# kv, the normalizer and kv Wo of a linear-attention block in one batch of small TensorE tiles, with the token sum on DVE

## The chip, the cores and the metric

The kernel runs on one core of one Trainium2 chip. The metric is device microseconds of one execution. Engines: PE is TensorE's matmul, PEld its weight load, DVE is VectorE, ACT is ScalarE, POOL is GpSimd.

## The reference, cut to what matters

```python
# A: linear attention, S = 2048 tokens, D = 512, 32 heads of 16
q, k, v = split(x @ wqkv)                       # per head
pq, pk = phi(q), phi(k)                         # phi(t) = where(t > 0, t + 1, exp(t)) + 1e-6
kv  = einsum("bhsd,bhse->bhde", pk, v)          # 16x16 per head
z   = einsum("bhsd->bhd", pk)                   # token sum of phi(k)
num = einsum("bhqd,bhde->bhqe", pq, kv)
den = einsum("bhqd,bhd->bhq", pq, z)[..., None] + 1e-6
a   = (num / den) @ wo
# B: a token-mixing MLP on layernorm(x), F = 1792 (the bulk of the matmuls: uacc, then yps)
out = g * a + (1 - g) * b
```

The kernel never forms v. It accumulates G = x^T pk (gacc), takes kv = wv^T G per head, folds kv with Wo into W2 = kv Wo (four blocks of 128 rows), and at the end computes pq W2 (aps). In the profile, kacc and qacc are x times the k and q columns of wqkv, and denps is den.

## The kernel before, in the parts that matter

```python
def mm(o, lhsT, rhs, start, stop, **kw):           # every matmul has this one line in the profile
    nc.tensor.matmul(o, lhsT=lhsT, rhs=rhs, start=start, stop=stop, **kw)

def kv_matmuls():                                  # 32 matmuls on 128x64 tiles
    kvps = bank("kvps")
    for j in range(ND):
        for k in range(ND):
            for h in (0, H2):                      # H2 = 64
                c = slice(j * P + h, j * P + h + H2)
                mm(kvps[h : h + H2, c], wv_sb[:, k, c], gT[:, k, c], k == 0, k == ND - 1,
                   tile_position=(0, h))
    for h in (0, H2):                              # keep the 16x16 blocks on the diagonal
        d = slice(h, h + H2)
        nc.vector.tensor_tensor(out=kvbdT[d, :, d], in0=kvps[d, :]..., in1=mask[d, d]..., op=ALU.mult)

def z_matmuls():                                   # sum over tokens: 8 matmuls against ones
    zps = bank("zps")
    for j in range(ND):
        for i, part in enumerate((zhi, zlo)):      # zacc split into two bf16 parts by DVE
            mm(zps[:, 8 * j : 8 * j + 8], part[:, j * P : (j + 1) * P], ones8[:], i == 0, i == 1)
    nc.vector.tensor_tensor(out=Z32..., in0=zps..., in1=maskH..., op=ALU.mult)

def w2_matmul(j):                                  # one full 128x128 matmul, 512 wide
    wps2 = bank("wps2")
    mm(wps2[:], kvbdT[:, j, :], wo_sb[:, j, :], True, True)
    nc.scalar.activation(out=W2sb[:, j, :], in_=wps2[:], func=ACT.Copy)

def den_matmuls():                                 # 16 matmuls on 128x32 tiles, 512 wide
    ...
    nc.vector.reciprocal(out=rden[:], in_=denps[:])

for j in range(NB0, NF):                           # NB0 = 3, NF = 14: one block of the MLP each
    for t in range(NT):                            # 16 matmuls of 128x512
        mm(acc[:], w1c[c][:, t, ...], hs[:, t, :], t == 0, t == NT - 1)
    gelu(j, acc)                                   # ACT
    if j == NB0 + 2:
        z_matmuls()
    if j == NB0 + 3:
        kv_matmuls()
        den_matmuls()
        gate_sums(); rden_chunk(0); rden_chunk(1)
    if NB0 + 5 <= j < NB0 + 5 + ND:
        w2_matmul(j - NB0 - 5)
    ...
```

Of the kernel before, what the change touches and what calls it, by code (L numbers as in the profile page):

```python
# [7 lines left out]
ACT = mybir.ActivationFunctionType  # L8
ALU = mybir.AluOpType
AX = mybir.AxisListType  # L10
BF16 = mybir.dt.bfloat16
FP32 = mybir.dt.float32
# [3 lines left out]
def kernel(  # L16
# [13 lines left out]
    nc = tc.nc  # L30
    P = nc.NUM_PARTITIONS
    EPS = 1e-5
    PHI_EPS = 1e-6
    HEAD = 16
# [3 lines left out]
    S, D = X.shape  # L38
    F = B_w1.shape[1]
    NT = S // P  # L40
    ND = D // P
# [2 lines left out]
    NSC = S // SC  # L44
    TPC = SC // P
    FB = 4
    assert S == 2048 and D == 512 and F % P == 0
    w1_chunks = [(j, min(FB, NF - j)) for j in range(0, NF, FB)]

# [14 lines left out]
    def keep(shape, dtype, name):  # L64
        return persist.tile(shape, dtype, name=name, tag=name)

    def bank(name, dtype=FP32):
        return ps.tile([P, SC], dtype, name=name, tag="bank")
# [6 lines left out]
    wv_sb = keep([P, ND, D], BF16, "wv_sb")  # L75
    wo_sb = keep([P, ND, D], BF16, "wo_sb")
    pqT = keep([P, ND, S], BF16, "pqT")
    pk = keep([P, NT, D], BF16, "pk")
    uT = keep([P, NF, D], BF16, "uT")
    kvbdT = keep([P, ND, P], BF16, "kvbdT")  # L80
    W2sb = keep([P, ND, D], BF16, "W2sb")
    Z32 = keep([P, ND * 40], BF16, "Z32")
    zhi = keep([P, D], BF16, "zhi")
    zlo = keep([P, D], BF16, "zlo")
    zacc = keep([P, D], FP32, "zacc")
    ones8 = nc.const_aps.tensor(1.0, (P, 8), BF16)
    rden = keep([P, SC], BF16, "rden")
    ident = keep([P, P], BF16, "ident")
    mask = keep([P, P], BF16, "mask")
    maskH = keep([P, 8], BF16, "maskH")  # L90
    gw_b = keep([P, D], BF16, "gw_b")
    brow = keep([P, P], BF16, "brow")
    bcol = keep([P, NF + NT], FP32, "bcol")
# [13 lines left out]
    def mm(o, lhsT, rhs, start, stop, **kw):  # L107
        nc.tensor.matmul(o, lhsT=lhsT, rhs=rhs, start=start, stop=stop, **kw)  # L108

    def block_mask(m, cols, width):  # L110
        nc.gpsimd.memset(m, 1.0)
        nc.gpsimd.affine_select(
            out=m, in_=m, compare_op=ALU.is_ge, fill=0.0, base=0,
            pattern=[[-HEAD, cols], [0, width]], channel_multiplier=1,
        )
        nc.gpsimd.affine_select(
            out=m, in_=m, compare_op=ALU.is_ge, fill=0.0, base=HEAD - 1,
            pattern=[[HEAD, cols], [0, width]], channel_multiplier=-1,
        )
# [29 lines left out]
    for c, (j0, nb) in enumerate(w1_chunks):  # L149
        w = wpool.tile([P, NT, FB * P], BF16, name="w1c", tag="wc")  # L150
        w1c.append(w)
        for t0 in range(0, NT, 8) if c == 0 else (0,):
            t1 = t0 + 8 if c == 0 else NT
            nc.sync.dma_start(
                out=w[:, t0:t1, : nb * P], in_=w1_view[:, t0:t1, j0 * P : (j0 + nb) * P]
# [5 lines left out]
    nc.vector.memset(ones_f[:], 1.0)  # L161
    nc.vector.memset(mhalf[:], -0.5)
    nc.vector.memset(Z32[:], 0.0)
    nc.vector.memset(kvbdT[:], 0.0)
    nc.gpsimd.memset(ident[:], 0.0)
    nc.gpsimd.affine_select(
        out=ident[:], in_=ident[:], compare_op=ALU.not_equal, fill=1.0, base=0,
        pattern=[[-1, P]], channel_multiplier=1,
    )
    block_mask(mask[:].rearrange("p (a b) -> p a b", b=HEAD), P // HEAD, HEAD)  # L170
    block_mask(maskH[:].rearrange("p (a b) -> p a b", b=1), 8, 1)

    nc.gpsimd.memset(brow[:], 0.0)

    def load_small():
# [92 lines left out]
    def z_add(t):  # L268
        first = pk[:, 0, :] if t == 1 else zacc[:]
        nc.vector.tensor_tensor(out=zacc[:], in0=first, in1=pk[:, t, :], op=ALU.add)  # L270
# [39 lines left out]
    gT = persist.tile([P, ND, D], BF16, name="gT", tag="wk_sb")  # L310
# [6 lines left out]
    def gelu(j, acc):  # L317
        nc.scalar.activation(  # L318
            out=uT[:, j, :], in_=acc[:], func=ACT.Gelu_apprx_tanh, bias=bcol[:, j : j + 1]
        )  # L320
# [3 lines left out]
        nc.tensor.transpose(pt[:, 0:P], brow[:], ident[:])  # L324
        nc.vector.tensor_copy(out=bcol[:], in_=pt[:, 0 : NF + NT])

    H2 = P // 2

    def kv_matmuls():
        kvps = bank("kvps")  # L330
        for j in range(ND):
            for k in range(ND):
                for h in (0, H2):
                    c = slice(j * P + h, j * P + h + H2)
                    mm(
                        kvps[h : h + H2, c], wv_sb[:, k, c], gT[:, k, c], k == 0, k == ND - 1,
                        tile_position=(0, h),
                    )
        for h in (0, H2):
            d = slice(h, h + H2)  # L340
            nc.vector.tensor_tensor(
                out=kvbdT[d, :, d],
                in0=kvps[d, :].rearrange("p (j d) -> p j d", j=ND)[:, :, d],
                in1=mask[d, d].unsqueeze(1).to_broadcast([H2, ND, H2]), op=ALU.mult,
            )

    def z_split():
        nc.vector.tensor_copy(out=zhi[:], in_=zacc[:])
        nc.vector.tensor_tensor(out=zlo[:], in0=zacc[:], in1=zhi[:], op=ALU.subtract)

    def z_matmuls():
        zps = bank("zps")
        for j in range(ND):
            for i, part in enumerate((zhi, zlo)):
                mm(
                    zps[:, 8 * j : 8 * j + 8], part[:, j * P : (j + 1) * P], ones8[:],
                    i == 0, i == 1,
                )
        nc.vector.tensor_tensor(
            out=Z32[:].rearrange("p (j m) -> p j m", m=40)[:, :, 0:8],  # L360
            in0=zps[:, 0:32].rearrange("p (j m) -> p j m", m=8),
            in1=maskH[:].unsqueeze(1).to_broadcast([P, ND, 8]), op=ALU.mult,
        )

    def w2_matmul(j):
        wps2 = bank("wps2")
        mm(wps2[:], kvbdT[:, j, :], wo_sb[:, j, :], True, True)
        nc.scalar.activation(out=W2sb[:, j, :], in_=wps2[:], func=ACT.Copy)

    def den_matmuls():  # L370
        denps = bank("denps")
        for j in range(ND):
            for c in range(NSC):
                mm(
                    denps[32 * c : 32 * c + 32, :], Z32[:, 32 * j : 32 * j + 32], pqT[:, j, c * SC : (c + 1) * SC],
                    j == 0, j == ND - 1, tile_position=(0, 32 * c),
                )
        with nc.allow_low_precision(reason="the normalizer is used in bf16"):
            nc.vector.reciprocal(out=rden[:], in_=denps[:])

    NB0 = 3
# [16 lines left out]
        gelu(jj, accs[jj])  # L398
    for t in range(11, NT):
        z_add(t)  # L400
    z_split()

    def gate_sums():
        for t in range(NT):
            junk = work.tile([P, D], BF16, name="junk", tag="junk", bufs=2)
            nc.vector.tensor_tensor_reduce(  # L406
                out=junk[:], in0=xs[:, t, :], in1=gw_b[:], scale=1.0, scalar=0.0,
                op0=ALU.mult, op1=ALU.add, accum_out=gpre[:, t : t + 1],
            )
# [3 lines left out]
    def rden_chunk(c):  # L413
        if c == 0:
            nc.gpsimd.dma_start(out=rd_dram[:], in_=rden[:])
        for j in range(ND):
            rex = work.tile([P, SC], BF16, name="rex", tag="rex", bufs=4)
            src = rd_dram[32 * c + 8 * j : 32 * c + 8 * j + 8, :]
            nc.gpsimd.dma_start(out=rex[:], in_=src.unsqueeze(1).to_broadcast([8, HEAD, SC]))  # L419
            seg = pqT[:, j, c * SC : (c + 1) * SC]  # L420
            nc.vector.tensor_tensor(out=seg, in0=seg, in1=rex[:], op=ALU.mult)  # L421
# [3 lines left out]
    def load_w2(c):  # L425
        w = wpool.tile([P, NT, FB * P], BF16, name="w2c", tag="wc")
        w2c.append(w)
        for f0 in (0, NF // 2):
            f1 = f0 + NF // 2
            nc.sync.dma_start(  # L430
                out=w[:, f0:f1, :], in_=w2_view[:, f0:f1, c * SC : (c + 1) * SC]
            )

    for j in range(NB0, NF):
        c, jj = divmod(j, FB)
        acc = bank("uacc")
        for t in range(NT):
            mm(acc[:], w1c[c][:, t, jj * P : (jj + 1) * P], hs[:, t, :], t == 0, t == NT - 1)
        gelu(j, acc)
        if j == NB0 + 2:  # L440
            z_matmuls()
        if j == NB0 + 3:
            kv_matmuls()
            den_matmuls()
            gate_sums()
            rden_chunk(0)
            rden_chunk(1)
        if NB0 + 5 <= j < NB0 + 5 + ND:
            w2_matmul(j - NB0 - 5)
        if jj == FB - 1 or j == NF - 1:  # L450
            load_w2(c)

# [2 lines left out]
        out=gg[:], in0=gth[:], scalar1=0.5, scalar2=0.5, op0=ALU.mult, op1=ALU.add  # L455
    )
    nc.vector.tensor_scalar(
        out=c1[:], in0=gth[:], scalar1=-0.5, scalar2=0.5, op0=ALU.mult, op1=ALU.add
# [3 lines left out]
    for t in range(NT):  # L462
        c, tl = divmod(t, TPC)
        aps = bank("aps")
        for j in range(ND):
# [3 lines left out]
            out=a_sc[:], in_=aps[:], func=ACT.Identity,  # L469
            scale=gg[:, t : t + 1], bias=c2[:, t : t + 1],  # L470
        )
        for c0, W in ((0, D - P), (D - P, P)) if t == NT - 1 else ((0, D),):
            cs = slice(c0, c0 + W)
            yps = bank("yps")
            for f in range(NF):
# [6 lines left out]
                out=ot[:, :W], in0=yps[:, :W], scalar=c1[:, t : t + 1], in1=a_sc[:, cs],  # L482
# [35 lines left out]
```

## Time and profile before

| | before |
|---|---|
| median of 3 runs | 165.23 us (165.11 to 165.82) |
| span of the profiled run | 163.4 us |
| PE busy | 158.7 us, 97% |
| granted clock | 1.0 |

A busy share alone says little about a pipelined engine, so the chain of waits is read with it. These are the busy line of the page and its chain that ended last, by engine and then by line:

```profile
PE 158.7 (97%) x787; PEld 73.3 (45%) x801; DVE 88.3 (54%) x202; ACT 58.7 (36%) x90; POOL 18.3 (11%) x37
...
PE 95%; DMA 2%; issue 1%; ACT 0%; DVE 0%
PE uacc L108 30%; PE yps L108 29%; PE aps L108 9%; PE gacc L108 8%; PE qacc L108 8%; PE kacc L108 8%; DMA xs<-in_A_x_dram 2%; PE pt L195 1%; PE denps L108 1%; PE wps L108 1%; PE kvps L108 0%; ACT xT L199 0%; DVE ot L481 0%; PE zps L108 0%; PE pt L324 0%
```

The chain lies on PE for 95% of the span: hardly anything but PE's own stream sets the time. What a change takes out of that stream is gained, as long as PE does not start to wait for something else.

The timeline of PE around the part that is changed follows. Its columns are the start in us from the start of the span, the time covered, the engine, the line, the operation, the output and its inputs, the tile and shape, and the count. The times of matmuls overlap (one of 512 columns has 0.38 us, and the next starts 0.216 us after it), so costs are read from one start to the next; such a step of 0.216 us is called a slot.

```profile
67.83 0.17 PE L108 MATMUL zps<-const-bfloat16-1.0,zhi 128*128 128x8 bf16 x1
...
68.01 0.17 PE L108 MATMUL zps<-const-bfloat16-1.0,zlo 128*128 128x8 bf16 x1
68.04 3.61 PE L108 MATMUL uacc<-hs,w1c 128*128 128x512 bf16 x16
71.58 0.69 PE L108 MATMUL kvps<-gT,wv_sb 128*64 128x64 bf16 x32
72.20 1.05 PE L108 MATMUL denps<-pqT,Z 128*32 128x512 bf16 x16
73.18 1.04 PE L108 MATMUL uacc<-hs,w1c 128*128 128x512 bf16 x3
```

From the start of zps to the next uacc 0.21 us pass. From the start of kvps to the uacc after denps 1.60 us pass, on tiles that are 64 columns wide in kvps and 32 in denps.

The same view further on shows kv Wo, named wps here, as one full matmul between the blocks of uacc, each costing one slot of 0.216 us (80.10 to 80.32). Two of the four are shown.

```profile
80.10 0.38 PE L108 MATMUL wps<-wo_sb,kvbdT 128*128 128x512 bf16 x1
80.32 3.62 PE L108 MATMUL uacc<-hs,w1c 128*128 128x512 bf16 x16
83.77 0.38 PE L108 MATMUL wps<-wo_sb,kvbdT 128*128 128x512 bf16 x1
```

The timeline of DVE over the same stretch shows the split of z, its mask, and the two mask instructions of kv. The bracket is the idle time before an instruction and what ended it.

```profile
64.08 0.43 DVE L348 CAST zhi<-zacc 128x512 bf16<-128x512 f32 x1
64.54 0.69 DVE L349 TENSOR_TENSOR zlo<-zacc,zhi 128x512 bf16<-128x512 f32 x1
68.22 0.19 DVE L359 TENSOR_TENSOR Z<-zps,maskH 128x32 bf16<-128x32 f32 x1 [2.98 <-PE zps L108]
72.32 0.86 DVE L341 TENSOR_TENSOR kvbdT<-kvps,mask 64x256 bf16<-64x256 f32 x2 [3.91 <-PE kvps L108]
73.31 3.36 DVE L379 RECIPROCAL rden<-denps 128x512 bf16<-128x512 f32 x1
```

### The profile page before, as it was taken

To read this page: it belongs to the slowest core of one execution; us is meant where nothing else is said; L and a number is where in the kernel's file an instruction comes from. 1 tells how busy PE (TensorE), PEld (TensorE's weight loads), DVE (VectorE), ACT (ScalarE), POOL (GpSimd) and SP (SyncE) were. 2 spreads that over 40 slices of the span, in tenths; PEclk is the share of its full clock that TensorE was granted. 3 is DMA by queue.
4 is the path that set the end of the run, shared out by engine and by line. 5 is a ranking of instruction groups with operands and counts; after the bars stand their busy time and mean duration, and the time that the engine had idled before them with its cause. 6 is when DMAs were issued, how large, how long until landed. Compare 5 with 4: busy or idle time off the path is not lost.

```text
span 163.4 us, 2099 instructions
## 1 busy us (share of the span) xinstructions
PE 158.7 (97%) x787; PEld 73.3 (45%) x801; DVE 88.3 (54%) x202; ACT 58.7 (36%) x90; POOL 18.3 (11%) x37
## 2 busy tenths in 40 slices
PE   7999999999999999999999999999999999999993
PEld 2544444444444444444444444444444444444452
DVE  1599999957999999029995301156221111111112
ACT  3463386648676483111222213111112222111110
POOL 5000711200100000001055500050000000000000
PEclk9999999999999999999999999999999999999999
DMA  5999999999950007600893599932100000111001
GB/s 152 235 237 213 280 308 328 349 349 348 326 130 0 0 0 247 202 4 0 286 299 101 181 320 279 323 121 88 36 32 32 32 32 32 45 52 35 32 32 32
DMA packets 30057, 25.05 MB, mean 153 GB/s; under 512 B 7968, under 2 KB 29472, under 8 KB 30048
## 3 DMA queue, kind: packets, MB, share of 16 engines
q1 hardware_dynamic: 28032, 22.02, 45.5%
q0 software_dynamic: 1440, 2.38, 5.5%
q10 hardware_dynamic: 576, 0.52, 1.1%
q8 instruction: 6, 0.10, 0.3%
q14 instruction: 3, 0.02, 0.0%
HBM read 21.11 MB, written 2.23 MB: 143 GB/s over the span
## 4 chain that ended last, share of the span: by engine, by line
PE 95%; DMA 2%; issue 1%; ACT 0%; DVE 0%
PE uacc L108 30%; PE yps L108 29%; PE aps L108 9%; PE gacc L108 8%; PE qacc L108 8%; PE kacc L108 8%; DMA xs<-in_A_x_dram 2%; PE pt L195 1%; PE denps L108 1%; PE wps L108 1%; PE kvps L108 0%; ACT xT L199 0%; DVE ot L481 0%; PE zps L108 0%; PE pt L324 0%
## 5 line engine op out<-in xcount | busy, mean ns | idle before, releaser
L108 PE MATMUL uacc<-hs,w1c 128*128 128x512 bf16 x219 | 51.8, 379 | 0.4
L108 PE MATMUL yps<-uT,w2c 128*128 128x512 bf16 (+2 forms) x234 | 50.6, 366 | 0.2
L481 DVE SCALAR_TENSOR_TENSOR ot<-yps,c,a_sc 128x512 bf16<-128x512 f32 (+2 forms) x17 | 12.2, 720 | 46.0 <-PE yps L108 42.7
L108 PEld LDWEIGHTS <-w2c 128*128 128x128 bf16 x238 | 22.8, 98 | 25.9
L108 PEld LDWEIGHTS <-w1c 128*128 128x128 bf16 x224 | 21.7, 98 | 26.3 <-issue 0.4
L468 ACT ACTIVATE a_sc<-aps,c,gg 128x512 f32<-128x512 f32 x16 | 12.4, 778 | 46.7 <-PE aps L108 43.0
L318 ACT ACTIVATE uT<-uacc,bcol 128x512 bf16<-128x512 f32 x14 | 9.3, 687 | 28.3 <-PE uacc L108 28.3
L108 PE MATMUL aps<-W2sb,pqT 128*128 128x512 bf16 x63 | 16.4, 379 | 0.1
L108 PE MATMUL qacc<-xT,wq_sb 128*128 128x512 bf16 x63 | 16.2, 379 | 0.0
L108 PE MATMUL kacc<-wk_sb,xT 128*128 128x512 bf16 x63 | 16.0, 380 | 0.1
L108 PE MATMUL gacc<-pk,xs 128*128 128x512 bf16 x62 | 15.5, 379 | 0.1
L245 ACT ACTIVATE hs<-xs,nmr,rstd 128x512 bf16<-128x512 bf16 x16 | 12.8, 805 | 1.9 <-DVE nmr L239 1.9
L205 ACT ACTIVATE e<-qacc 128x512 bf16<-128x512 f32 x16 | 9.6, 597 | 9.2 <-PE qacc L108 8.3
L419 POOL DMA_DIRECT2D rex<-rd_dram x16 | 9.4, 602 | 23.0 <-DVE pqT L421 17.5
L205 ACT ACTIVATE e<-kacc 128x512 bf16<-128x512 f32 x16 | 9.3, 595 | 6.9 <-PE kacc L108 5.6
L209 DVE SCALAR_TENSOR_TENSOR pk<-kacc,e 128x512 bf16<-128x512 f32 x16 | 11.1, 692 | 0.6
L209 DVE SCALAR_TENSOR_TENSOR pqT<-qacc,e 128x512 bf16<-128x512 f32 x16 | 11.1, 692 | 0.6
L229 DVE BATCH_NORM_STATS2 stats<-xs 128x6 f32<-128x512 bf16 x16 | 10.9, 682 | 0.0
L206 DVE TENSOR_SCALAR e<-e 128x512 bf16<-128x512 bf16 x32 | 9.0, 282 | 3.1 <-ACT e L205 3.1
L406 DVE CUSTOM_DVE_ANT_0 junk<-xs,gw_b 128x512 bf16<-128x512 bf16 x16 | 9.9, 684 | 0.0
L270 DVE TENSOR_TENSOR zacc<-zacc,pk 128x512 f32<-128x512 f32 x14 | 9.6, 686 | 0.2
L108 PEld LDWEIGHTS <-pqT 128*128 128x128 bf16 x64 | 6.3, 98 | 7.6
(65 smaller groups left out, 69.6 us busy)
## 6 DMA issues: line engine op xcount, KB each, us to landing
w2c<-in_B_w_dram SPq DMA_DIRECT2D x8, 896.0 KB, 6.6
w1c<-in_B_w_dram SPq DMA_DIRECT2D x2, 2048.0 KB, 15.7
w1c<-in_B_w_dram SPq DMA_DIRECT2D x3, 1024.0 KB, 12.9
rex<-rd_dram POOLq DMA_DIRECT2D x16, 128.0 KB, 3.2
out_dram<-ot SPq DMA_DIRECT2D x15, 128.0 KB, 1.7
xs<-in_A_x_dram SPq DMA_DIRECT2D x3, 512.0 KB, 5.1
wq_sb<-in_A_wqkv_dram SPq DMA_DIRECT2D x1, 512.0 KB, 7.1
wv_sb<-in_A_wqkv_dram SPq DMA_DIRECT2D x1, 512.0 KB, 11.4
```

Source lines behind the costliest of these rows:

```text
L108: nc.tensor.matmul(o, lhsT=lhsT, rhs=rhs, start=start, stop=stop, **kw)
L205: nc.scalar.activation(out=e[:], in_=acc[:], func=ACT.Exp)
L206: nc.vector.tensor_scalar(out=e[:], in0=e[:], scalar1=1.0, scalar2=PHI_EPS, op0=ALU.min, op1=ALU.add)
L209: nc.vector.scalar_tensor_tensor(out=dst, in0=acc[:], scalar=0.0, in1=e[:], op0=ALU.max, op1=ALU.add)
L229: nc.vector.bn_stats(out=stats[:], in_=xs[:, t, :])
L245: nc.scalar.activation(out=hs[:, t, :], in_=xs[:, t, :], func=ACT.Identity, scale=rstd[:, t : t + 1], bias=nmr[:, t : t + 1],)
L270: nc.vector.tensor_tensor(out=zacc[:], in0=first, in1=pk[:, t, :], op=ALU.add)
L318: nc.scalar.activation(out=uT[:, j, :], in_=acc[:], func=ACT.Gelu_apprx_tanh, bias=bcol[:, j : j + 1])
L406: nc.vector.tensor_tensor_reduce(out=junk[:], in0=xs[:, t, :], in1=gw_b[:], scale=1.0, scalar=0.0, op0=ALU.mult, op1=ALU.add, accum_out=gp ...
L419: nc.gpsimd.dma_start(out=rex[:], in_=src.unsqueeze(1).to_broadcast([8, HEAD, SC]))
L468: nc.scalar.activation(out=a_sc[:], in_=aps[:], func=ACT.Identity, scale=gg[:, t : t + 1], bias=c2[:, t : t + 1],)
L481: nc.vector.scalar_tensor_tensor(out=ot[:, :W], in0=yps[:, :W], scalar=c1[:, t : t + 1], in1=a_sc[:, cs], op0=ALU.mult, op1=ALU.add,)
```

## The change

The intent is to take matmul slots out of PE's stream. The token sum is finished on DVE (a 32x32-block transpose, two reductions and small copies) instead of by eight matmuls. kv is computed in 32-column tiles, so that kvps and denps use the same tile shape. kv Wo becomes sixteen matmuls on the sixteen different 32x32 tiles of the array, which can run at once: block i of group j goes to row tile i and column tile i XOR j of bank j (a bank is the result buffer that bank() hands out). Its results come out permuted by 32 partitions, and ACT's copies put them back, with eleven copies instead of four.

```diff
     def kv_matmuls():
         kvps = bank("kvps")
         for j in range(ND):
             for k in range(ND):
-                for h in (0, H2):
-                    c = slice(j * P + h, j * P + h + H2)
-                    mm(kvps[h : h + H2, c], wv_sb[:, k, c], gT[:, k, c], ..., tile_position=(0, h))
+                for q in range(0, P, Q32):
+                    c = slice(j * P + q, j * P + q + Q32)
+                    mm(kvps[q : q + Q32, j * Q32 : (j + 1) * Q32], wv_sb[:, k, c], gT[:, k, c],
+                       ..., tile_position=(0, q))
-        (two masked copies of 64x256 into kvbdT)
+        (one masked copy of 128x128 into kvT)
 
-    def z_split(): ...            # zhi, zlo
-    def z_matmuls(): ...          # 8 matmuls
+    def z_column():
+        nc.vector.transpose(out=zT[:], in_=zacc[:])
+        nc.vector.tensor_reduce(out=zpart[:], in_=zT[:]..., op=ALU.add, axis=AX.X)
+        (4 copies of 32x16, a reduction, 4 copies of 32x4)
         nc.vector.tensor_tensor(out=Z32..., in1=maskH..., op=ALU.mult)
 
-    def w2_matmul(j): ...
+    def w2_matmuls():
+        w2ps.extend(bank("w2ps") for _ in range(ND))
+        for j in range(ND):
+            for i in range(NQ):
+                r, c = i * Q32, (i ^ j) * Q32
+                mm(w2ps[j][c : c + Q32, :], kvT[r : r + Q32, j, :], wo_sb[r : r + Q32, j, :],
+                   True, True, tile_position=(r, c))
+    def w2_copies(j):             # 1, 4, 2 and 4 ACT copies for j = 0 to 3
...
-        if j == NB0 + 2:
-            z_matmuls()
         if j == NB0 + 3:
             kv_matmuls()
             den_matmuls()
+            w2_matmuls()
...
-        if NB0 + 5 <= j < NB0 + 5 + ND:
-            w2_matmul(j - NB0 - 5)
+        if NB0 + 3 <= j < NB0 + 3 + ND:
+            w2_copies(j - NB0 - 3)
```

The set-up loses a memset on DVE and three mask instructions on POOL, and gains a small reduction on DVE. Some names in the diff are shortened.

More of the change, by code (lines that the diff above doesn't have):

```diff
@@ L46 @@
     FB = 4
+    Q32 = 32
+    NQ = P // Q32
+    NZ = D // Q32
     assert S == 2048 and D == 512 and F % P == 0
@@ L79 @@
     uT = keep([P, NF, D], BF16, "uT")
-    kvbdT = keep([P, ND, P], BF16, "kvbdT")
+    kvT = keep([P, ND, Q32], BF16, "kvT")
     W2sb = keep([P, ND, D], BF16, "W2sb")
     Z32 = keep([P, ND * 40], BF16, "Z32")
-    zhi = keep([P, D], BF16, "zhi")
-    zlo = keep([P, D], BF16, "zlo")
     zacc = keep([P, D], FP32, "zacc")
-    ones8 = nc.const_aps.tensor(1.0, (P, 8), BF16)
+    zT = keep([P, D], FP32, "zT")
+    zpart = keep([P, NZ], FP32, "zpart")
+    zquad = keep([Q32, NQ, NZ], FP32, "zquad")
+    zsum = keep([Q32, NZ], FP32, "zsum")
+    zcol = keep([P, ND], FP32, "zcol")
     rden = keep([P, SC], BF16, "rden")
     ident = keep([P, P], BF16, "ident")
-    mask = keep([P, P], BF16, "mask")
     maskH = keep([P, 8], BF16, "maskH")
+    maskQ = keep([P, 2], BF16, "maskQ")
     gw_b = keep([P, D], BF16, "gw_b")
@@ L163 @@
     nc.vector.memset(Z32[:], 0.0)
-    nc.vector.memset(kvbdT[:], 0.0)
     nc.gpsimd.memset(ident[:], 0.0)
@@ L169 @@
     )
-    block_mask(mask[:].rearrange("p (a b) -> p a b", b=HEAD), P // HEAD, HEAD)
     block_mask(maskH[:].rearrange("p (a b) -> p a b", b=1), 8, 1)
+    nc.vector.tensor_reduce(
+        out=maskQ[:], in_=maskH[:].rearrange("p (a m) -> p m a", m=2), op=ALU.max, axis=AX.X
+    )
     nc.gpsimd.memset(brow[:], 0.0)
@@ L325, in biases @@
         nc.vector.tensor_copy(out=bcol[:], in_=pt[:, 0 : NF + NT])
-    H2 = P // 2
     def kv_matmuls():
@@ L332, in kv_matmuls @@
             for k in range(ND):
-                for h in (0, H2):
-                    c = slice(j * P + h, j * P + h + H2)
-                    mm(
-                        kvps[h : h + H2, c], wv_sb[:, k, c], gT[:, k, c], k == 0, k == ND - 1,
-                        tile_position=(0, h),
-                    )
-        for h in (0, H2):
-            d = slice(h, h + H2)
-            nc.vector.tensor_tensor(
-                out=kvbdT[d, :, d],
-                in0=kvps[d, :].rearrange("p (j d) -> p j d", j=ND)[:, :, d],
-                in1=mask[d, d].unsqueeze(1).to_broadcast([H2, ND, H2]), op=ALU.mult,
-            )
@@ L347, in z_split @@
-    def z_split():
-        nc.vector.tensor_copy(out=zhi[:], in_=zacc[:])
-        nc.vector.tensor_tensor(out=zlo[:], in0=zacc[:], in1=zhi[:], op=ALU.subtract)
-    def z_matmuls():
-        zps = bank("zps")
-        for j in range(ND):
-            for i, part in enumerate((zhi, zlo)):
-                mm(
-                    zps[:, 8 * j : 8 * j + 8], part[:, j * P : (j + 1) * P], ones8[:],
-                    i == 0, i == 1,
-                )
+                for q in range(0, P, Q32):
+                    c = slice(j * P + q, j * P + q + Q32)
+                    mm(
+                        kvps[q : q + Q32, j * Q32 : (j + 1) * Q32], wv_sb[:, k, c], gT[:, k, c],
+                        k == 0, k == ND - 1, tile_position=(0, q),
+                    )
@@ new lines, in kv_matmuls @@
+        nc.vector.tensor_tensor(
+            out=kvT[:].rearrange("p j (m d) -> p j m d", d=HEAD),
+            in0=kvps[:, 0 : ND * Q32].rearrange("p (j m d) -> p j m d", j=ND, d=HEAD),
+            in1=maskQ[:].unsqueeze(1).unsqueeze(3).to_broadcast([P, ND, 2, HEAD]), op=ALU.mult,
+        )
+    def z_column():
+        nc.vector.transpose(out=zT[:], in_=zacc[:])
+        nc.vector.tensor_reduce(
+            out=zpart[:], in_=zT[:].rearrange("p (b k) -> p b k", k=Q32), op=ALU.add, axis=AX.X
+        )
+        for q in range(NQ):
+            nc.vector.tensor_copy(out=zquad[:, q, :], in_=zpart[q * Q32 : (q + 1) * Q32, :])
+        nc.vector.tensor_reduce(
+            out=zsum[:], in_=zquad[:].rearrange("p q b -> p b q"), op=ALU.add, axis=AX.X
+        )
+        for q in range(NQ):
+            nc.vector.tensor_copy(
+                out=zcol[q * Q32 : (q + 1) * Q32, :],
+                in_=zsum[:].rearrange("p (j q) -> p q j", q=NQ)[:, q, :],
+            )
@@ L359, in z_matmuls @@
         nc.vector.tensor_tensor(
             out=Z32[:].rearrange("p (j m) -> p j m", m=40)[:, :, 0:8],
-            in0=zps[:, 0:32].rearrange("p (j m) -> p j m", m=8),
+            in0=zcol[:].unsqueeze(2).to_broadcast([P, ND, 8]),
             in1=maskH[:].unsqueeze(1).to_broadcast([P, ND, 8]), op=ALU.mult,
         )
-    def w2_matmul(j):
-        wps2 = bank("wps2")
-        mm(wps2[:], kvbdT[:, j, :], wo_sb[:, j, :], True, True)
-        nc.scalar.activation(out=W2sb[:, j, :], in_=wps2[:], func=ACT.Copy)
+    w2ps = []
@@ new lines, in w2_matmuls @@
+    def w2_matmuls():
[3 more added lines that the diff above has]
+                r, c = i * Q32, (i ^ j) * Q32
+                mm(
+                    w2ps[j][c : c + Q32, :], kvT[r : r + Q32, j, :], wo_sb[r : r + Q32, j, :],
+                    True, True, tile_position=(r, c),
+                )
+    def w2_copies(j):
+        n = Q32 * (NQ, 1, 2, 1)[j]
+        for r in range(0, P, n):
+            c = (r // Q32 ^ j) * Q32
+            nc.scalar.activation(
+                out=W2sb[r : r + n, j, :], in_=w2ps[j][c : c + n, :], func=ACT.Copy
+            )
@@ L400 @@
         z_add(t)
-    z_split()
+    z_column()
     def gate_sums():
```

## The prediction

> **What bounds the kernel now.** TensorE. The page gives PE 158.7 us busy of a 163.4 us span, the chain of waits puts 95% of the span on PE, and the granted clock is 1.0. From 5 us to 160.6 us the chain is one unbroken row of matmuls. So the change is worth what it takes out of PE's stream, if no new wait opens. The part touched is small: in the timeline, zps holds PE from 67.83 to 68.04 us, kvps and denps from 71.58 to 73.18 us, and four full matmuls of kv Wo one 0.216 us slot each.
>
> **Costs, from the starts of PE's instructions in the trace.**
> - A 128x512 matmul follows the last after 0.216 us.
> - zps: eight matmuls, 25.5 ns apart. All removed (the token sum goes to DVE): **-0.21 us**.
> - kvps: 16 pairs of 128x64 tiles, 32 ns a pair: 0.50 us. After: 16 groups of four 128x32 tiles. Tiles in different columns start about 3 ns apart (denps: four within 10 ns, rounds 0.216 us apart), so I estimate 25 to 32 ns per group: **-0.05 us**.
> - kv Wo: 4 x 0.216 = 0.86 us removed. After: sixteen 32x32 tiles, all different, each (bank, 32 partitions) written once. The Trainium skill (TensorE: Matmul & The Clock Gate, "Measured speedup vs the span model") reports 10.6x for 16 such tiles; no run here shows them yet. With 3.3 ns per start I estimate 0.216 + 16 x 3.3 ns = 0.27 us: **-0.59 us**.
> - Changes of tile shape cost about 0.1 us each (uacc to kvps 309 ns less 216; kvps to denps 126 less 32; denps to uacc 322 less 216). That agrees with the skill's page TensorEngine Tiling (Array Packing), "Key Properties": a change of mode drains TensorE. Before: three. After: kvps and denps share 128x32, then 32x32, then 128x128: three again, **0**.
>
> Sum about -0.85 us, all on the critical path.
>
> **Off the path.**
> - DVE loses the split of z (0.43 + 0.69 us) and half of the kv mask, and gains a 128x512 transpose, a reduction and ten tiny instructions: an estimated 3 us from 64.1 us. denps needs it near 72: 4 us of slack.
> - kvT: an estimated 0.3 us on DVE after kvps, while denps holds PE for 0.96 us: kv Wo should not wait.
> - ACT: 11 copies for 4 at about 0.59 us: +4.1 us. The worst block, gelu 0.69 plus four copies 2.35, fits in one uacc block (3.45 us). Last copy near 87 us; aps starts near 97.
> - The last scaled pqT is ready near 93 us: slack remains.
>
> **Prediction: 164.4 us** (-0.5%), 80% range 163.9 to 165.2. Chances: faster by over 2%: 0.01; within 2%: 0.97; slower: 0.02.
>
> **What would show it right or wrong.** zps gone; kvps about 0.45 us; denps following kvps without the 0.09 us gap; w2ps within 0.3 us of starts; no PE idle "until DVE"; the first aps about 0.85 us earlier (97.4); everything after it shifted equally.
>
> **What would make it wrong.** (a) The sixteen w2ps tiles serialise by rows or banks: 0.86 us, and the gain falls to 0.3. (b) PE is fed too slowly: 128 + 32 + 32 instructions within 1.8 us, double today's burst; a limit per instruction would cost 1 us or more. (c) kv Wo waits for kvT. (d) ACT's copies delay a gelu and with it a bank.

## The result, and the profile after

The changed kernel took 164.50 us (median of 6 runs, 163.88 to 164.69) against 165.57 us (6 runs) of the kernel before. The ratio is 0.9934, 95% interval 0.9912 to 0.9956. A ratio is the mean time of one kernel's fast runs over that of the other's fast runs of the same rounds, so it is not quite the ratio of the medians.

The page after, same lines:

```profile
PE 158.0 (97%) x823; PEld 72.9 (45%) x837; DVE 89.5 (55%) x210; ACT 63.3 (39%) x97; POOL 17.5 (11%) x34
...
PE 96%; DMA 2%; issue 1%; DVE 0%
PE uacc L113 30%; PE yps L113 30%; PE kacc L113 9%; PE aps L113 8%; PE gacc L113 8%; PE qacc L113 8%; DMA xs<-in_A_x_dram 2%; PE pt L201 1%; PE denps L113 1%; PE kvps L113 0%; PE w2ps L113 0%; DVE ot L500 0%; PE pt L330 0%
```

The limit is still PE: zps and wps are gone from the chain, and w2ps appears in it. The timeline of PE in the same stretch:

```profile
65.65 5.77 PE L113 MATMUL uacc<-hs,w1c 128*128 128x512 bf16 x26
71.36 0.66 PE L113 MATMUL kvps<-gT,wv_sb 128*32 128x32 bf16 x64
71.84 1.06 PE L113 MATMUL denps<-pqT,Z 128*32 128x512 bf16 x16
72.83 0.43 PE L113 MATMUL w2ps<-wo_sb,kvT 32*32 32x512 bf16 x16
73.19 1.04 PE L113 MATMUL uacc<-hs,w1c 128*128 128x512 bf16 x3
```

The uacc matmuls now run on without a break where zps stood. From the start of kvps to the next uacc 1.84 us pass instead of 1.60, and in return four slots of 0.216 us and zps's 0.20 us are gone. The timeline of DVE:

```profile
64.05 0.71 DVE L350 STREAM_TRANSPOSE zT<-zacc 128x512 f32<-128x512 f32 x1
64.79 0.69 DVE L351 TENSOR_REDUCE zpart<-zT 128x16 f32<-128x512 f32 x1
65.51 0.69 DVE L355 COPY zquad<-zpart 32x16 f32<-32x16 f32 x4
66.24 0.25 DVE L356 TENSOR_REDUCE zsum<-zquad 32x16 f32<-32x64 f32 x1
66.52 0.68 DVE L360 COPY zcol<-zsum 32x4 f32<-32x4 f32 x4
67.24 0.20 DVE L364 TENSOR_TENSOR Z<-zcol,maskH 128x32 bf16<-128x32 f32 x1
72.11 0.29 DVE L343 TENSOR_TENSOR kvT<-kvps,maskQ 128x128 bf16<-128x128 f32 x1 [4.67 <-PE kvps L113]
```

The new chain on DVE runs from 64.05 to 67.44 us (67.24 plus 0.20). denps, which needs it, starts at 71.84, so 4.4 us are to spare. The mask of kv takes 0.29 us. The timeline of ACT, first lines of the copies:

```profile
76.86 0.69 ACT L324 ACTIVATE uT<-uacc,bcol 128x512 bf16<-128x512 f32 x1 [2.99 <-PE uacc L113]
77.57 2.39 ACT L386 ACTIVATE W2sb<-w2ps 32x512 bf16<-32x512 f32 x4
80.31 0.69 ACT L324 ACTIVATE uT<-uacc,bcol 128x512 bf16<-128x512 f32 x1 [0.36 <-PE uacc L113]
```

Four copies of 32x512 take 2.39 us, as long as four of 128x512 would at 0.59 each. They fit between two gelus with 0.36 us of idle time left.

**Where the time came from.** In all fourteen profiles the start of the first uacc scatters between 32.69 and 33.64 us, while the stretch from the first aps to the last yps matmul is 62.139 or 62.140 us and the tail after it 3.06 to 3.09 us. So the stretch from the first uacc to the first aps, which holds the whole change after set-up, is the fine measure here:

| us | before | after | difference |
|---|---|---|---|
| first uacc to first aps | 64.986 | 64.161 | -0.825 |
| last uacc before kvps, to kvps | 0.309 | 0.310 | 0 |
| kvps, first to last start | 0.499 (32 matmuls) | 0.477 (64) | -0.022 |
| last kvps to first denps | 0.126 | 0.009 | -0.117 |
| denps, first to last start | 0.667 | 0.679 | +0.012 |
| last denps to first uacc | 0.312 | 0.310 + 0.050 + 0.315 (with w2ps between) | +0.363 |
| four wps slots | 0.864 | 0 | -0.864 |
| zps | 0.203 | 0 | -0.203 |

All are differences of starts of single instructions in the trace. The lines add up to the total within 6 ns.

### The profile page after: what moved, and what is told of

The parts are those of the page before. It is cut to its first block, busy times and chain, and to the rows that moved or that the text cites. A ratio compares the mean times of both kernels' runs of the same rounds, so it can differ in the third digit from the quotient of the medians.

```text
span 162.6 us, 2183 instructions
## 1 busy us (share of the span) xinstructions
PE 158.0 (97%) x823; PEld 72.9 (45%) x837; DVE 89.5 (55%) x210; ACT 63.3 (39%) x97; POOL 17.5 (11%) x34
## 4 chain that ended last, share of the span: by engine, by line
PE 96%; DMA 2%; issue 1%; DVE 0%
PE uacc L113 30%; PE yps L113 30%; PE kacc L113 9%; PE aps L113 8%; PE gacc L113 8%; PE qacc L113 8%; DMA xs<-in_A_x_dram 2%; PE pt L201 1%; PE denps L113 1%; PE kvps L113 0%; PE w2ps L113 0%; DVE ot L500 0%; PE pt L330 0%
## 5 line engine op out<-in xcount | busy, mean ns | idle before, releaser
L113 PE MATMUL uacc<-hs,w1c 128*128 128x512 bf16 x219 | 51.0, 379 | 0.4
```

## The experiments

Twelve kernels ran, all with correct results. "Stretch" is first uacc to first aps in the profiled run.

| run | median us (before, same rounds) | ratio, 95% interval | stretch us |
|---|---|---|---|
| before | | | 64.986 |
| after | 164.50 (165.57) | 0.9934, 0.9912 to 0.9956 | 64.161 |
| a0_after_again | 164.23 (165.54) | 0.9918, 0.9905 to 0.9931 | 64.160 |
| a1_z_only | 165.44 (165.54) | 0.9987, 0.9974 to 1.0001 | 64.788 |
| a2_kv_only | 165.28 (165.54) | 0.9981, 0.9967 to 0.9994 | 64.861 |
| a3_w2_only | 165.05 (165.54) | 0.9972, 0.9957 to 0.9987 | 64.553 |
| b1_full_batch | 165.57 (165.69) | 0.9996, 0.9979 to 1.0012 | 65.038 |
| b2_diagonal | 165.28 (165.69) | 0.9969, 0.9939 to 0.9999 | 64.767 |
| b3_w2_twice | 164.60 (165.69) | 0.9935, 0.9918 to 0.9952 | 64.375 |
| b4_kv_twice | 166.76 (165.69) | 1.0065, 1.0049 to 1.0080 | 66.187 |
| b5_kv_twice_shifted | 165.76 (165.43) | 1.0020, 1.0001 to 1.0039 | 65.696 |
| c1_den_first | 164.67 (165.43) | 0.9954, 0.9933 to 0.9975 | 64.669 |
| c2_after_old_start | 164.82 (165.43) | 0.9961, 0.9944 to 0.9978 | 64.161 |
| c3_before_new_start | 165.56 (165.43) | 1.0005, 0.9985 to 1.0024 | 64.987 |

### The whole and its three parts

The control, a0_after_again, has no edit.

> The changed kernel once more, as control for the three partial kernels of this call. Theory (PE slots): the gain is the time taken out of TensorE's stream, 0.85 us at the first aps in the trace of the result, so 0.995 of before. Rival (something outside the stream, such as the start or the tail, gives part of the 1.07 us between the medians): the ratio stays near 0.993 while the first aps moves by only 0.85 us.

The stretch repeats to 0.001 us (64.160). The ratio does not settle so well: 0.9918, whose interval excludes the 0.995 that the stretch alone gives. Runs c2 and c3 take this up.

a1_z_only, from the kernel before:

```diff
-    z_split()                     # and z_matmuls() at j == NB0 + 2
+    z_column()
```

> The kernel before with only the token sum moved to DVE (eight zps matmuls gone). Theory: -0.20 us, the zps slot (0.419 us between the uacc matmuls around it, less the 0.216 that follow any such matmul); first aps at about 98.0 us instead of 98.23; no PE wait on DVE, as the DVE chain ends near 67.5 us and denps needs it near 72. Rival: DVE's longer chain (3.4 us instead of 1.1) gives some of it back.

Stretch 64.788, that is -0.198 us; the ratio agrees (0.9987). DVE's longer chain gave nothing back.

a2_kv_only, from the kernel before:

```diff
-                for h in (0, H2):
+                for q in range(0, P, Q32):      # 64 tiles of 128x32; mask by four DVE instructions
```

> The kernel before with only kv in 64 tiles of 32 columns (mask applied by four DVE instructions, which nothing waits for here). Theory: kvps start to denps start falls from 0.625 to about 0.486 us, -0.14: nearly all from the gap of 0.126 us before denps, since both now use 128x32 tiles, and almost none from the matmuls themselves (0.499 to 0.477). Rival: the smaller tiles are what is faster, and the gap before denps stays near 0.1 us.

Stretch 64.861, that is -0.125 us. The timeline of PE in this run:

```profile
71.28 0.66 PE L109 MATMUL kvps<-gT,wv_sb 128*32 128x32 bf16 x64
71.77 1.06 PE L109 MATMUL denps<-pqT,Z 128*32 128x512 bf16 x16
```

From the start of kvps to the start of denps 0.49 us pass instead of 0.62. The gap before denps fell from 0.126 to 0.008 us, the matmuls themselves only from 0.499 to 0.478. So the gain is not from the smaller tiles as such, but from the change of tile shape that is no longer there. c1 below, with the two batches in the other order, agrees: from the last denps to the first kvps 0.206 us pass, no more than from one round of four denps to the next.

a3_w2_only, from the kernel before:

```diff
+                mm(w2ps[j][c : c + Q32, :], kvbdT[r : r + Q32, j, r : r + Q32],
+                   wo_sb[r : r + Q32, j, :], True, True, tile_position=(r, c))
```

> The kernel before with only kv Wo as sixteen 32x32 tiles behind denps (weights cut from the same block-diagonal tile). Theory: four slots of 0.216 us go (-0.864), the batch with one more change of tile shape comes (+0.36): -0.50 us, less at most 0.05 because the two mask instructions end just as denps does. Rival (the batch is worth nothing by itself, only together with the 32-column kv): 0. The three parts should add up to the whole: -0.20 -0.14 -0.50 = -0.84 us.

Stretch 64.553, that is -0.433 us. The timeline of PE:

```profile
72.54 1.05 PE L110 MATMUL denps<-pqT,Z 128*32 128x512 bf16 x16
73.52 0.50 PE L110 MATMUL w2ps<-wo_sb,kvbdT 32*32 32x512 bf16 x16
```

In this run the second mask instruction ends at 73.525 us, when w2ps has already begun; the third w2ps matmul, the first that needs it, starts 0.056 us after that, and the starts of w2ps span 0.114 us instead of 0.050. The 0.064 us more account for nearly all that the parts lack: -0.198 - 0.125 - 0.433 = -0.756 against -0.825 for the whole.

### Batch or concurrency

b1_full_batch, from the kernel before:

```diff
+    def w2_matmuls():
+        w2ps.extend(bank("w2ps") for _ in range(ND))
+        for j in range(ND):
+            mm(w2ps[j][:], kvbdT[:, j, :], wo_sb[:, j, :], True, True)   # right after den_matmuls()
```

> The kernel before with its four full 128x128 kv Wo matmuls in one batch behind denps, no tiling. Theory (tiles running at once give the gain, not the batching): the same time as before, 0 to +0.05 us at the first aps. Rival (batching gives the gain, by fewer interruptions of uacc): about -0.5 us.

Stretch 65.038, +0.052 us: batching alone gives nothing, and costs the wait for the mask.

b2_diagonal, from the changed kernel:

```diff
-                r, c = i * Q32, (i ^ j) * Q32
+                r, c = i * Q32, i * Q32          # and four plain copies of 128x512
```

> The changed kernel with block i of kv Wo always in tile (i, i): sixteen matmuls on four tiles instead of sixteen, with plain 128x512 copies (four instead of eleven). Theory: four rounds of 0.216 us, so +0.65 us at the first aps against the changed kernel, and total near 0.85 - 0.65 = 0.2 us under before. Rival 1 (what counts is the number of small matmuls, not distinct tiles): no change. Rival 2 (the ACT copies cost time): faster than the changed kernel, as seven copies of 0.59 us are gone.

Stretch 64.767, +0.606 us against the changed kernel. The line of w2ps in the timeline of PE:

```profile
72.30 1.04 PE L113 MATMUL w2ps<-wo_sb,kvT 32*32 32x512 bf16 x16
```

The same sixteen matmuls on four tiles instead of sixteen span 0.669 us of starts instead of 0.050, that is four rounds instead of one. The XOR is what brings the gain of kv Wo. The starts of w2ps account for the whole difference (+0.619), so dropping seven ACT copies bought nothing.

b3_w2_twice, from the changed kernel:

```diff
-            w2_matmuls()
+            w2_matmuls(2)                        # every matmul of the batch issued twice, same result
```

> The changed kernel with the kv Wo batch issued twice (same result). Theory: the second batch adds one round, +0.22 us at the first aps, and no further change of shape. Rival (sixteen tiles run one row group or one bank after another, hidden in the modelled ends): +0.5 to +0.9 us. Rival 2 (issue, 32 more instructions at some 4 ns each, overlapping the first round): nearly 0.

The lines of w2ps and of the next uacc in the timeline of PE:

```profile
72.98 0.65 PE L113 MATMUL w2ps<-wo_sb,kvT 32*32 32x512 bf16 x32
73.56 0.61 PE L113 MATMUL uacc<-hs,w1c 128*128 128x512 bf16 x2
```

Stretch 64.375, +0.214 us: sixteen more matmuls cost one 512-wide slot. The sixteen tiles do run at once; serialisation hidden behind the modelled ends of matmuls is excluded.

### How fast PE is fed

In the changed kernel the starts of kvps show two paces. The first 32 matmuls come in groups of four every 25 ns, the other 32 one by one every 8.3 ns, which is 33 ns per four.

b4_kv_twice, from the changed kernel:

```diff
-        for j in range(ND):
+        for j in [j for j in range(ND) for _ in range(2)]:   # in kv_matmuls
```

> The changed kernel with every kv tile computed twice, 128 small matmuls for 64 (each repetition starts its sum anew, the result is the same). In the changed kernel the first 32 of them run as groups of four every 25 ns, the other 32 one every 8.3 ns. Theory (the first 64 instructions were waiting ready, after that PE is fed one matmul with its weight load per 8.3 ns): groups of four up to the 32nd, then 96 at 8.3 ns: +0.53 us. Rival (the array itself sets 25 ns per group, the slower half belongs to the blocks j = 2 and 3): the change of pace comes at the 64th matmul, +0.47 us. Rival 2: 25 ns per group throughout, +0.40 us.

The pace changed again after the 32nd matmul, and 96 matmuls followed at 8.3 ns: kvps took 1.011 us, +0.534, as the theory had it. In c1 below, where kvps follows denps, the pace changes after the 28th kvps matmul, which with the last round of four denps makes 32 again. That these 32 were waiting ready is the reading that fits; no view shows the waiting itself. But the stretch grew by 2.026 us. The timeline of PE shows where the rest went:

```profile
71.69 1.20 PE L113 MATMUL kvps<-gT,wv_sb 128*32 128x32 bf16 x128
72.71 1.06 PE L113 MATMUL denps<-pqT,Z 128*32 128x512 bf16 x16
73.69 0.41 PE L113 MATMUL w2ps<-wo_sb,kvT 32*32 32x512 bf16 x7
75.21 0.41 PE L113 MATMUL w2ps<-wo_sb,kvT 32*32 32x512 bf16 x9 [1.11 <-issue]
75.56 0.82 PE L113 MATMUL uacc<-hs,w1c 128*128 128x512 bf16 x3
```

Within w2ps the 8th matmul starts 1.50 us after the 7th (the 1.11 us of the line leave out the time of the 7th), "issue" being time in which it waited for nothing that the profile shows. Nobody had expected this. The record of DMA packets has an instruction fetch of 16384 bytes that starts at 72.82 us and takes 1.15 us. It ends 1.24 us before the resumption at 75.21; no view shows what fills that time. The Trainium skill (Runtime: NRT & Kernel Launch, "Instruction fetch mechanics") says that instructions are refilled in blocks of 16 KiB, 256 instructions. In the profile of a3 the last four such fetches start when 661, 919, 1173 and 1431 of PE's matmuls and weight loads have started, about 256 apart. In b4 655 of them precede kvps, so the fetch due near 660 fell into the beginning of the burst (it starts 1.13 us after kvps), and 957 precede the matmul that came late, some 300 on. kvps twice, denps and w2ps are 320 instructions within 2 us, where the uacc blocks have 32 in 3.45 us.

b5_kv_twice_shifted, from b4:

```diff
+        if j == NB0:
+            pad = bank("pad")
+            for _ in range(40):
+                mm(pad[:, 0:8], warm[:, 0:P], warm[:, 0:8], True, True)
```

> The kernel with every kv tile computed twice lost 1.50 us inside its kv Wo batch, between the 7th and the 8th matmul, while an instruction fetch of 16384 bytes [...] was under way from 72.81 us; nobody had predicted that. Theory: TensorE had used up the instructions it held; the fetch was started only some 250 instructions earlier, just as the burst began. Here 40 tiny matmuls (8 columns, 80 instructions with their weight loads) stand three uacc blocks earlier, so that the same fetch comes some 9 us before the burst. Expected: the 1.50 us stall is gone (the w2ps starts lie within 0.06 us), kvps still takes 1.01 us, the pad costs about 1.0 us, and the whole is about 0.5 us faster than the unshifted one. Rival (a stall from the waits or banks of the batch, tied to the program and not to the fetch): it stays at 1.50 us.

```profile
72.53 1.20 PE L113 MATMUL kvps<-gT,wv_sb 128*32 128x32 bf16 x128
73.55 1.06 PE L113 MATMUL denps<-pqT,Z 128*32 128x512 bf16 x16
74.53 0.43 PE L113 MATMUL w2ps<-wo_sb,kvT 32*32 32x512 bf16 x16
```

The stall is gone: the starts of w2ps span 0.050 us again, with the same 1.011 us of kvps, and the fetch now starts at 67.24 us, 5 us before kvps (9 were expected; and in b4 it started 1.13 us into the burst, not "just as the burst began"). The stretch is 0.491 us shorter than in b4, although the pad costs about 1.0 us. So the stall belongs to where the burst lies against the blocks of instructions, not to the batch itself; that PE had run out of instructions is the theory that fits, not something that a view names (the pad also takes a bank of its own, which nothing waits for). The exact moment at which PE asks for a block was not measured. The changed kernel's own burst is 128 + 32 + 32 = 192 instructions, less than one block, and neither of its two profiles shows the stall, although the fetch falls into the burst there too, 1.01 and 1.08 us after the start of kvps. So it does in b3 (1.24 us), with 224 instructions and no stall. With the fetch in this place, then, 224 instructions did not stall and 320 did.

### A named wait that is none, and one that is

The changed kernel's timeline of weight loads names DVE as what ended the idle time before kv Wo:

```profile
71.83 0.57 PEld L113 LDWEIGHTS <-Z 128*32 128x32 bf16 x16
72.83 0.14 PEld L113 LDWEIGHTS <-kvT 32*32 32x32 bf16 x16 [0.42 <-DVE kvT L343]
```

c1_den_first, from the changed kernel:

```diff
-            kv_matmuls()
-            den_matmuls()
-            w2_matmuls()
+            denps = den_matmuls()
+            kv_matmuls()
+            w2_matmuls()
+            den_reciprocal(denps)
```

> The changed kernel with denps ahead of kvps, so that nothing but the mask lies between kvps and kv Wo. Theory: in the changed kernel the mask ends at 72.40 us, 0.43 us before w2ps starts, and only the change of tile shape holds w2ps (the view that names DVE as its releaser is wrong). Here the wait becomes real: last kvps start to first w2ps about 0.6 us (end of kvps 0.18, to DVE 0.1, mask 0.29, back 0.06) and the aps comes 0.4 to 0.55 us later than in the changed kernel. Rival (w2ps waits for DVE in the changed kernel as well, with a long way from DVE to PE): the wait after the mask ends is 0.43 us here too, last kvps to w2ps about 1.0 us, and aps 0.9 us later.

```profile
71.86 0.79 PEld L113 LDWEIGHTS <-wv_sb 128*32 128x32 bf16 x64
72.83 0.29 DVE L343 TENSOR_TENSOR kvT<-kvps,maskQ 128x128 bf16<-128x128 f32 x1 [5.55 <-PE kvps L113]
73.17 0.14 PEld L113 LDWEIGHTS <-kvT 32*32 32x32 bf16 x16 [0.53 <-DVE kvT L343]
```

Both lines of kvT's weight loads name DVE, with 0.42 and 0.53 us. In c1 the mask ends at 73.121 us and w2ps starts 0.054 us later: that wait is real. In the changed kernel the mask ends at 72.399 us and w2ps starts 0.431 us later, 0.310 us after the last start of denps, which lies within the 0.306 to 0.318 us that every other change of shape behind a 512-wide matmul takes in these profiles where nothing else is waited for. The mask was not what held it. The stretch of c1 is 0.508 us longer, as expected; denps in front of kv Wo hides the mask.

### The set-up

c2_after_old_start and c3_before_new_start exchange the set-up of the two kernels:

```diff
 # c2, from the changed kernel: unused, as before
+    nc.vector.memset(kvbdT[:], 0.0)
+    block_mask(mask[:]..., P // HEAD, HEAD)
 # c3, from the kernel before: moved
-    nc.vector.memset(kvbdT[:], 0.0)            # both go to where the small loads are issued
-    block_mask(mask[:]..., P // HEAD, HEAD)
```

> The changed kernel with the old set-up work put back unused (three mask instructions on GpSimd, a memset on DVE). The medians fell by 1.07 and 1.31 us in two sets, TensorE's stream from the first uacc to the last yps only by 0.83. Theory: the rest is scatter of the start, where the first uacc came anywhere from 32.7 to 33.6 us in ten profiles of both families; then this equals the changed kernel, ratio about 0.992 to 0.995 of before. Rival: the shorter set-up is worth the other 0.3 us; then this is at 0.995 or above and its first uacc comes later.

> The kernel before with its set-up shortened as in the changed one (mask and memset moved to where the small loads are issued, work otherwise unchanged). Theory: no change, ratio within 0.0015 of 1. Rival: 0.3 us faster, 0.998.

The stretches are those of their families to 0.001 us. c3 gave nothing (1.0005). c2 came out at 0.9961, above the range of the theory and where the rival had put it, but its interval reaches down to 0.9944, and its first uacc (33.51 us) lies within the scatter, as does that of a0 (33.64 us) with the short set-up. The two runs disagree on the rival. All runs together lean to it. If the stretch of a kernel's profile holds for all its executions, then the mean time less the stretch is below that of the kernel before, in the same rounds, by 0.12 to 0.47 us in each of the seven kernels with the new set-up (after, a0, b2, b3, b4, b5, c1; 0.35 on average); in the five with the old one (a1, a2, a3, b1, c2) it differs by -0.20 to +0.15. In c3, which moves the old work instead of dropping it, it differs by +0.04. So some 0.3 us outside the stretch seem to go with the new set-up; which part of it brings them is not shown. Three sets of the same stream gave 0.9934, 0.9918 and 0.9961; the stretch alone gives 0.995.

No run beat the changed kernel by its stretch.

## Why the prediction was right

- **Bound by PE, nothing given back.** Right. The first aps came at 97.4 us as forecast (luck in part: the profiles of before and after happen to start uacc within 0.03 us of each other; in a0, the same kernel, the first aps comes at 97.80), and from it to the last yps the length stayed the same to 0.001 us. The change took 0.825 us out of the stream; 0.85 was forecast.
- **zps, -0.21.** Right: -0.198 by itself (a1).
- **kv Wo, -0.59, before changes of shape.** Right. Sixteen tiles cost one slot (b3, +0.214) plus 0.050 us of starts, 3.3 ns each. With its one more change of shape the part is worth -0.50 (0.363 - 0.864). It needs all sixteen tiles (b2) and is not a matter of batching (b1). The 10.6x that the prediction quotes was not measured: no run has the sixteen one after another on a single tile.
- **Changes of shape, 0 net.** Right. The one between kvps and denps is gone (-0.117), the one between denps and w2ps is new (0.310 less the 0.216 of the matmul before it: 0.094). By starts, denps to uacc in the kernel before is 312 ns, not the 322 of the prediction; that does not touch the sum.
- **kvps, -0.05.** The size was off: -0.022. The estimate of 25 to 32 ns per group of four held for the first 32 matmuls only; after them the pace is 8.3 ns each, 33 ns per four. This is warning (b) of the prediction, a limit per instruction. It was there, but cost less than 0.1 us, not "1 us or more". b4 shows that a longer burst can lose more: 1.50 us, which goes away when the blocks of instructions are shifted (b5).
- **DVE, 3 us.** It took 3.4 us, with 4.4 us of slack.
- **kvT and ACT do not hold PE.** Right for both (c1 and the stretch). The expected sign "no PE idle until DVE" did fail literally, since the view names DVE before kv Wo; the times of the mask show that it had long been done.
- **The total.** 164.5 us against 164.4 forecast, which is closer than the reasoning earned. The forecast started from 165.23 us, the median of three runs; the six runs beside the changed kernel gave 165.57, 0.34 more, and the medians fell by 1.07 us, not by 0.85. The two differences partly cancel, and that is luck. What supports the forecast is the stretch, -0.825 us. The start scatters by up to 0.95 us between profiles; the share outside the stretch, which seems to go with the set-up, was not forecast, and its cause is open.

## What to carry to other kernels

When PE is the limit, count slots from start to start: a small change in the stream can be predicted to some hundredths of a microsecond, and the same stretch in two traces shows it where medians do not. Sixteen 32x32 products cost one 512-wide slot only if they use sixteen different tiles, and each change of tile shape cost about 0.1 us here, so order batches by shape and put work on the same engine between a result and its use. Keep a burst of tiny matmuls short: two instructions per matmul add up. The burst of 320 instructions in b4 lost 1.50 us, more than its 128 kvps matmuls took (1.011), where bursts of 192 and 224 lost nothing.

## What the Trainium skill lacked or had wrong

- TensorEngine Tiling (Array Packing), "Gotcha 1: PSUM Pressure", says that different row tiles cannot access the same PSUM bank simultaneously. Here the four row tiles of one j write one bank, in four different ranges of 32 partitions, with starts within 10 ns; a whole second batch costs 0.214 us (b3) and the results are correct. Its "Key Properties" give no figure for a change of mode. Here it costs 0.09 to 0.10 us beyond the slot of the 512-wide matmul before it, and the gap falls from 0.126 to 0.008 us when two batches share a shape (a2).
- TensorE: Matmul & The Clock Gate, "Measured speedup vs the span model", gives about 4 ns per tile; here 3.3 ns. The table at the head of the page gives a queue depth of 64 for TensorE, which agrees with the change of pace after 32 matmuls with their weight loads. The pace after that, 8.3 ns per matmul with its load, is on no page; the 62 ns per matmul that the page gives for decoding without hardware is not what is seen here.
- Runtime: NRT & Kernel Launch, "Instruction fetch mechanics", says that fetching is hidden because instructions are issued more slowly than they arrive. The blocks of 256 agree with the fetches of 16384 bytes in the trace, but a burst of 320 instructions in 2 us was stalled for 1.50 us (b4), and not after the blocks were shifted (b5); that it waited for a fetch is inferred from these two runs.
